# Scales carried between partitions by a DMA transpose instead of TensorE, in a three-stage kernel of attention and a Fourier mix

## The chip, the cores and the metric

One core of a Trainium2 chip. The metric is the device time of one execution, in microseconds (us). Engines are named as in the profile: PE is TensorE (PEld its weight loads), DVE is VectorE, ACT is ScalarE, POOL is GpSimd, and SP is the engine that issues nearly all DMAs, in the order of its own queue.

## The reference

Two independent results are concatenated. The first is a sliding-window attention over 2048 tokens with 32 heads of 32, the second a two-dimensional Fourier transform of another input, written as matrix products:

```python
qkv = (x @ wqkv)                                   # 2048 x 1024 by 1024 x 3072
scores = einsum("bhqd,bhkd->bhqk", q, k) * Dh**-0.5
mask = (i - j >= 0) & (i - j < 256)
a = (softmax(where(mask, scores, -1e9)) @ v) @ wo
re = x_B @ dft_hid_re.T;  im = x_B @ dft_hid_im.T
b = dft_seq_re @ re - dft_seq_im @ im              # 2048 x 2048 by 2048 x 1024
return concatenate([a, b], axis=-1)
```

All inputs are 32-bit floats.

## The kernel before

Every large product is done with 16-bit floats, three matmuls for one: an operand is multiplied by a scale, rounded to a high half, and what is left becomes a low half (`split`: ScalarE writes the high half, VectorE the low one). The scale is one number for a block of an operand, the reciprocal of a power of two just at or below its largest (or largest mean) absolute value. So ahead of each `split` four steps come:

- `top` (VectorE, a maximum) or `mean` (ScalarE, a sum of absolute values; `u_top` does the same for the Fourier matrices) leaves one number for each of the 128 partitions in `tops[key]`.
- `spread` takes the maximum over the pieces of a block, still one for each partition.
- `scale_of` brings the 128 numbers into every partition: a TensorE transpose of the column, repeated 128 times, against the identity `ident` writes a 128x128 tile `pt` in PSUM, and VectorE takes the maximum of its rows.
- three small operations on VectorE follow: keep the exponent (an `and` with 0x7F800000), bound and shift it, take the reciprocal.

The work goes in three stages. In the first, `order` lists 96 products (q, k and v of the attention, in chunks), and `tasks` lists by `at(n, ...)` what is written ahead of product n: loads, tops, scales, splits. `w_finish` is the scale and split of a block of the q or k weights, `wv_scale` and `wv_split` those of the v weights, `xp_step`, `scan_scale` those of the Fourier input and matrices and of the output weights. In the second stage 48 units of seven products each (`seven`, whose positions 0 to 6 use the PSUM banks a b a c a b a) do the Fourier transform: 16 of kind x, and 32 of kind c, whose operands `un_a`, `un_b`, `un_c` are split by `u_step` with the scale from `u_scale`. `u_top` runs two units ahead (turns 0 and 2), `u_scale` at the last turn of that unit. In the third stage the attention's output weights are applied.

Beside the first two stages the attention runs block by block (256 of them), fed by `tick`: `s_step` writes scores `s`, VectorE the row maximum `mx` and later the low half `hl`, ScalarE `bias`, the exponentials and the high half; one DMA transpose on SP turns `hl` into `t`, GpSimd masks it, and `v_step` multiplies it by v six blocks later.

TensorE's matmuls are chained in program order by `mm`. The order on the other engines is made when the kernel is built, by a scheduler with a model of times; `tc.issue_after(x)` pins an instruction behind another one on its engine. `behind[0]` is VectorE's latest low half of the attention, of q, k or v, or its latest addition in `seven`; `line[0]` is SP's latest transpose of `hl` or pinned load.

`pa` is the pool of the first stage; its tiles `yq` and `yv` (two buffers each) hold the results of q, k and v until their DMA has stored them.

Of the kernel before, what the change touches and what calls it, by code (L numbers as in the profile page):

```python
# [9 lines left out]
F32 = mybir.dt.float32  # L10
F32R = mybir.dt.float32r
F16 = mybir.dt.float16
BF16 = mybir.dt.bfloat16
U8 = mybir.dt.uint8
U32 = mybir.dt.uint32
AF = mybir.ActivationFunctionType
ALU = mybir.AluOpType
AX = mybir.AxisListType

P = 128  # L20
S = 2048
D = 1024
H = 32
# [5 lines left out]
CH = 512  # L29
NCH = S // CH  # L30
QB = CH // P
VW = 2 * DH + 2
# [8 lines left out]
VW = 2 * DH + 2  # L41
# [12 lines left out]
def fused_kernel(ctx: ExitStack, tc: tile.TileContext, xa, wqk, wv, wo, xb, wd, cs, out):  # L54
    nc = tc.nc
# [8 lines left out]
    const = ctx.enter_context(tc.tile_pool(name="const", bufs=1))  # L64
# [4 lines left out]
    ps_v = ctx.enter_context(tc.tile_pool(name="ps_v", bufs=1, space=PSUM))  # L69
# [8 lines left out]
    tsum = reg1[:, :7 * 8 * CH].rearrange("p (s h k c) -> p s h k c", s=7, h=2, k=4)  # L78
    spare = reg1[:, 7 * 8 * CH:]

    ident = const.tile([P, P], F32, name="ident")
    make_identity(nc, ident)


    upper = const.tile([P, P], F32, name="upper")
# [2 lines left out]
                            fill=0.0, base=0, pattern=[[1, P]], channel_multiplier=-1)  # L88
    upper2 = upper.bitcast(U32).unsqueeze(1).to_broadcast([P, 2, P])
    never = const.tile([P, 1], F32, name="never")  # L90
# [3 lines left out]
    pshift = const.tile([P, 1], F32, name="pshift")  # L94
    nc.gpsimd.memset(pshift, PSHIFT)

    nbank, units_on = [0], []

    def bank(name):
        nbank[0] += 1  # L100
        return ps_m.tile([P, CH], F32, tag=f"m{nbank[0] % 3}", name=name)
# [6 lines left out]

    junk = const.tile([P, ND * P], U8, name="junk")
    fixed = []  # L110
# [22 lines left out]
        return const.tile([P, 2], F32, name=f"sc_{name}")  # L133

    tops, head = {}, [True]


    behind = []
# [18 lines left out]
    def spread(key, n):  # L157
        t = tops.pop(key)
        if n > 1:
            t1 = small.tile([P, 1], F32, tag="top0", name=f"top1_{key}")  # L160
            vec(nc.vector.tensor_reduce, t1, t, axis=AX.X, op=ALU.max)
        else:
            t1 = t
        tops[key] = t1

    def scale_of(key, v, s, down=2.0 ** -14):

        if head[0]:
            pt = ps_s.tile([P, CH], F32, tag="s", name=f"pt_{key}")[:, :P]
            with tc.issue_after(fixed[0].ins) if fixed else nullcontext():  # L170
                fixed[:] = [nc.tensor.transpose(pt, tops.pop(key).to_broadcast([P, P]), ident)]
        else:
            pt = (ps_v.tile([P, CH], F32, tag="pv", name=f"pt_{key}") if units_on else bank(f"pt_{key}"))[:, :P]
            nc.tensor.transpose(pt, tops.pop(key).to_broadcast([P, P]), ident)
        vec(nc.vector.tensor_reduce, v, pt, axis=AX.X, op=ALU.max)
        vec(nc.vector.tensor_scalar, v.bitcast(U32), v.bitcast(U32), 0x7F800000, None, op0=ALU.bitwise_and)
        vec(nc.vector.tensor_scalar, v, v, 2.0 ** -100, down, op0=ALU.max, op1=ALU.mult)
        vec(nc.vector.reciprocal, s, v)
# [25 lines left out]
    line = []  # L204
# [193 lines left out]
    def at(n, f, *args):  # L398
        tasks.setdefault(n, []).append((f, args))
# [22 lines left out]
    def w_top(kd, g):  # L422
        mean(f"w{kd}{g}", wraw[kd, g].rearrange("p d t -> p (d t)"), 0, 1)
        spread(f"w{kd}{g}", 1)
# [126 lines left out]
    for (kd, g), n in use.items():  # L551
        if kd in "qk" and n >= 4:
            at(n - 6, w_load, kd, g)
            at(n - 4, w_top, kd, g)
            at(n - 3, w_finish, kd, g)
    for g in range(NG):
        at(max(use["q", g], use["k", g], 11), scores_scale, g)

# [3 lines left out]
        at(n, x_split, 0, (i,), behind_act)  # L562
    at(7, strict.__setitem__, 0, False)
    at(7, head.__setitem__, 0, False)
    at(4, x_top, 2, (0, 1))
    at(5, x_top, 2, (2, 3))
    at(7, x_finish, 2)
# [4 lines left out]
    at(11, x_known)  # L572
    at(11, wv_load, 0)
    at(14, wv_top, 0)
    at(15, wv_scale, 0)
    for i, n in enumerate((15, 16, 16, 17)):
        at(n, wv_split, 0, (i,))
    at(15, wv_load, 1)
    at(18, wv_top, 1)
    at(19, wv_scale, 1)  # L580
    for i, n in enumerate((19, 20, 21, 21)):
        at(n, wv_split, 1, (i,))
    at(20, wv_known)
    def scan(key, ns):
# [292 lines left out]
    at(len(order) - 3, x_left, 0, "c")  # L877


    with tc.tile_pool(name="pa", bufs=2) as pa:  # L880
        def qk_out(kd, g, c, ps, f):
            y = pa.tile([P, 2, CH], F16, tag="yq", name=f"y{kd}{g}_{c}")
            behind_act[:] = [nc.scalar.activation(y[:, 0], ps, AF.Copy, scale=f)]
            behind[:] = [vec(nc.vector.scalar_tensor_tensor, y[:, 1], ps, f, y[:, 0],
                             op0=ALU.mult, op1=ALU.subtract)]
            a = "qk".index(kd)
            nc.sync.dma_start(qk[g, c, a:a + 2, :, :, a].rearrange("j d h t -> (d h) j t"), y)
            nc.sync.dma_start(qk[g, c, 2 - 2 * a, :, :, a].rearrange("d h t -> (d h) t"), y[:, 0])

        def d_out(g):  # L890
            qk_out("q", g, 0, direct.pop(g), f0[:, g:g + 1])

        w_top("q", 0)
        x_top(0, (0, 1, 2, 3))
        d_mm(0, range(0, 4))
        w_scale("q", 0)
        d_mm(0, range(4, 8))
        w_top("q", 1)
        d_mm(1, range(0, 1))
        x_scale(0)  # L900
        d_known(0)
        d_mm(1, range(1, 3))
        w_scale("q", 1)
        d_known(1)
        d_out(0)
        w_split("q", 0)
        w_top("q", 2)
        d_mm(1, range(3, 8))
        x_top(1, (0, 1))
        d_out(1)  # L910
        d_mm(2, range(0, 2))
        w_scale("q", 2)
        d_known(2)
        x_top(1, (2, 3))
        d_mm(2, range(2, 8))
        w_top("q", 3)
        d_mm(3, range(0, 2))
        x_scale(1)
        x_split(1, (0, 1))
        d_out(2)  # L920
        d_mm(3, range(2, 4))
        w_scale("q", 3)
        d_known(3)
        x_split(1, (2,))
        d_mm(3, range(4, 8))
        x_split(1, (3,))
        w_split("q", 1)
        d_out(3)

        for n, (kd, g, c) in enumerate(order):  # L930
            if n < 4:
                continue
            if n == 22:
                first_cm.__exit__(None, None, None)
                att_cm = tc.tile_pool(name="att", bufs=2, side="right")
                cell["att"] = att_cm.__enter__()
                agen[0] = attention()
                upcoming[0] = next(agen[0])
            for f, args in tasks.pop(n, ()):
                f(*args)  # L940
            rate[0] = 2 * early * EARLY.get(n, 0.85) / 24
            ps = bank(f"p{kd}{g}_{c}")
            if kd == "v":
                t = c
                product(ps, lambda h, d: xin[:, t // 4, h, d, t % 4 * P:t % 4 * P + P],
                        lambda h, d: reg2[:, g, h, d])
                y = pa.tile([P, H // 2, VW], F16, tag="yv", name=f"yv{g}_{t}")
                nc.gpsimd.memset(y[:, :, DH:DH + 1], 1.0)
                nc.gpsimd.memset(y[:, :, 2 * DH + 1:], 0.0)
                f = vf[:, g, t // 4:t // 4 + 1]  # L950
                pv = ps.rearrange("p (h d) -> p h d", d=DH)
                behind_act[:] = [nc.scalar.activation(y[:, :, :DH], pv, AF.Copy, scale=f)]
                behind[:] = [nc.vector.scalar_tensor_tensor(y[:, :, DH + 1:2 * DH + 1], pv, f, y[:, :, :DH],
                                                            op0=ALU.mult, op1=ALU.subtract)]
                nc.sync.dma_start(vs[t, :, g * (H // 2) * VW:(g + 1) * (H // 2) * VW],
                                  y.rearrange("p h w -> p (h w)"))
            else:
                u = wun[kd, g]
                product(ps, lambda h, d: u[:, h, d], lambda h, d: xin[:, c, h, d])
                qk_out(kd, g, c, ps, DOWN if kd == "q" else kf[:, c:c + 1])  # L960
            if kd == "v" and g == 0 and c % 4 == 3:
                ready.add((0, c // 4))
            if kd == "v" and g == 1 and c == NT - 1:
                pass
            if kd == "k" and g > 0:
                ready.add((g, c))
# [116 lines left out]
            hook(pos)  # L1083


    units_on.append(True)
    perm, turns = [(nbank[0] + 1 + k) % 3 for k in range(3)], [0]
    with tc.tile_pool(name="pb", bufs=1) as pb:
        ybufs = [pb.tile([P, 2, CH], F32, name=f"y{k}") for k in range(3)]
        ybufs.append(spare[:, 16 * P:].bitcast(F32).rearrange("p (e c) -> p e c", e=2))  # L1090
        ny = [0]
# [11 lines left out]
        for r in range(4):  # L1103
            x0, c0 = 12 * r, 12 * r + 4
            for j in range(4):
                n = x0 + j
# [5 lines left out]
            for j in range(8):  # L1112
                n = c0 + j
# [20 lines left out]
        for n, (kind, p, c, i) in enumerate(units):  # L1134
# [35 lines left out]
            f = fu.pop(n)  # L1170
# [16 lines left out]
        for q in range(NT // 2):  # L1187
# [5 lines left out]
                  lambda t, y, at_=0: nc.sync.dma_start(out[t * P:t * P + P, at_:at_ + y.shape[1] * y.shape[2]],  # L1193
                                                        y.rearrange("p e c -> p (e c)")),
# [51 lines left out]
```

## Time and profile before

| | us |
|---|---|
| median of 3 runs | 1708.01 |
| lowest and highest | 1707.69, 1711.28 |
| the profiled execution | 1705.92 |
| its span, first to last instruction | 1703.9 |
| DVE, ACT, POOL busy | 1301.6, 1169.3, 573.8 |

The page also gives 348.62 MB moved by DMA, and a granted TensorE clock of 1.000 throughout. The busy time of PE is modelled from pipelined matmuls, whose durations overlap; the time that a matmul takes from the queue is read from the starts of its neighbours.

### The profile page before, as it was taken

What the parts mean: (1) busy time and instruction counts of PE and PEld (TensorE: products, weight loads), DVE (VectorE), ACT (ScalarE), POOL (GpSimd) and SP (SyncE); (2) the same over time, 40 slices, a digit from 0 to 9 for tenths busy, and PEclk for the clock granted to TensorE, in tenths of its full rate; (3) what the DMA queues carried; (4) which work ended last, traced back from release to release, by engine and by line L of the source; (5) the groups of instructions that cost most, each with busy time, mean ns of one, the idle gap of its engine ahead of it and who ended that gap; (6) DMA issues with size and microseconds to landing.
All of it is one profiled execution on the core that took longest, in us unless ns stands there. A gap on an engine that the chain in (4) does not pass through costs nothing.

```text
span 1703.9 us, 30860 instructions
## 1 busy us (share of the span) xinstructions
PE 1693.1 (99%) x10999; PEld 851.4 (50%) x10999; DVE 1301.6 (76%) x2225; ACT 1169.3 (69%) x2035; POOL 573.8 (34%) x874
## 2 busy tenths in 40 slices
PE   9999999999999999999999999999999999999999
PEld 4444555555555554555555555555555555444444
DVE  6847788887988688887678886688886698688442
ACT  4466666676877687888678886678877687563322
POOL 0000322334444341444423474433555425411000
PEclk9999999999999999999999999999999999999999
DMA  9747999999998995887998999986999976876431
GB/s 351 244 138 241 258 289 273 289 254 305 249 231 218 207 231 122 197 203 178 226 249 246 198 183 175 232 201 120 194 167 203 228 183 136 173 184 119 116 99 75
DMA packets 469898, 348.62 MB, mean 205 GB/s; under 512 B 376944, under 2 KB 409968, under 8 KB 468848
## 3 DMA queue, kind: packets, MB, share of 16 engines
q1 hardware_dynamic: 462064, 321.48, 75.3%
q0 software_dynamic: 7680, 25.17, 9.2%
q8 instruction: 86, 1.41, 0.4%
q14 instruction: 68, 0.56, 0.1%
HBM read 166.99 MB, written 106.17 MB: 160 GB/s over the span
## 4 chain that ended last, share of the span: by engine, by line
PE 80%; DVE 7%; ACT 4%; DMA 4%; issue 3%; POOL 2%; SPq 0%; DVEq 0%; POOLq 0%; ACTq 0%
PE p_a L114 22%; PE pv L114 13%; PE p_b L114 10%; PE pk L114 9%; PE pq L114 8%; PE p_c L114 5%; PE po_a L114 5%; PE s L114 3%; PE po_b L114 2%; PE far L114 1%; PE po_c L114 1%; DMA t<-hl 1%; DMA ots<-ot 1%; DVE reg L835 1%; DVE hl L270 1%
## 5 line engine op out<-in xcount | busy, mean ns | idle before, releaser
L266 ACT ACTIVATE s<-s,bias,escs 128x256 f32<-128x256 f32 (+1 forms) x512 | 270.0, 528 | 11.7
L284 POOL TENSOR_SCALAR_AFFINE_SELECT z<-t 128x512 f16<-128x512 f16 x224 | 187.0, 841 | 159.6 <-PE pv L114 142.3
L259 ACT ACTIVATE bias<-mx,pshift,escs 128x2 f32<-128x2 f32 x256 | 98.3, 384 | 171.6 <-DVE mx L256 171.3
L270 DVE TENSOR_TENSOR hl<-s,hl 128x512 f16<-128x512 f32 (+1 forms) x256 | 170.1, 665 | 56.0 <-ACT hl L269 55.2
L114 PEld LDWEIGHTS <-reg 128*128 128x128 f16 x1344 | 128.9, 97 | 141.7
L286 POOL TENSOR_SCALAR_AFFINE_SELECT t<-t 128x512 f16<-128x512 f16 x224 | 183.8, 829 | 11.4
L114 PE MATMUL p_a<-reg,un_c 128*128 128x512 f16 x768 | 181.2, 379 | 0.4 <-ACT p_c L1068 0.2
L263 POOL TENSOR_SCALAR mark<-bias 128x1 f32<-128x1 f32 x128 | 53.1, 415 | 363.0 <-ACT bias L259 356.5
L114 PE MATMUL pk<-reg,wu_k 128*128 128x512 f16 x768 | 174.4, 379 | 0.0
L256 DVE TENSOR_REDUCE mx<-s 128x2 f32<-128x512 f32 (+1 forms) x256 | 170.9, 668 | 3.4
L114 PE MATMUL pv<-reg,reg 128*128 128x512 f16 x768 | 172.7, 379 | 0.0
L114 PEld LDWEIGHTS <-un_c 128*128 128x128 f16 x1152 | 109.9, 97 | 121.3 <-issue 2.0
L114 PEld LDWEIGHTS <-un_b 128*128 128x128 f16 x1152 | 110.0, 97 | 117.8 <-issue 1.1
L114 PEld LDWEIGHTS <-un_a 128*128 128x128 f16 x1152 | 109.7, 97 | 116.3
L269 ACT ACTIVATE hl<-s 128x512 f16<-128x512 f32 (+1 forms) x256 | 148.8, 581 | 6.4 <-DMA t<-hl 1.0
L114 PE MATMUL pq<-reg,wu_q 128*128 128x512 f16 x672 | 151.3, 379 | 0.8 <-DVE reg L121 0.5
L114 PE MATMUL p_a<-reg,un_b 128*128 128x512 f16 x576 | 136.4, 379 | 0.4 <-DVE y L1036 0.3
L114 PE MATMUL p_b<-reg,un_b 128*128 128x512 f16 x576 | 136.4, 379 | 0.3 <-DVE reg L835 0.3
L114 PE MATMUL p_a<-reg,un_a 128*128 128x512 f16 x576 | 136.6, 379 | 0.0
L114 PE MATMUL p_c<-reg,un_a 128*128 128x512 f16 x576 | 136.5, 379 | 0.0
L254 DVE COPY_PREDICATED s<-upper,far 128x256 f32<-128x256 uint32 x224 | 94.3, 421 | 46.2 <-PE s L114 44.9
L114 PEld LDWEIGHTS <-qk 96*128 96x128 f16 x1056 | 87.9, 97 | 64.3 <-issue 1.8
(208 smaller groups left out, 3153.2 us busy)
## 6 DMA issues: line engine op xcount, KB each, us to landing
raw_u<-in_cs_dram SPq DMA_DIRECT2D x64, 512.0 KB, 4.9
qk<-qk SPq DMA_DIRECT2D x64, 384.0 KB, 4.9
out_dram<-y POOLq DMA_DIRECT2D x72, 256.0 KB, 6.1
raw_wd<-in_wd_dram SPq DMA_DIRECT2D x24, 512.0 KB, 5.2
vs<-yv SPq DMA_DIRECT2D x32, 264.0 KB, 4.4
vt<-vs SPq DMA_DIRECT2D x64, 132.0 KB, 4.5
raw_wo<-in_wo_dram SPq DMA_DIRECT2D x16, 512.0 KB, 8.1
qk<-yq SPq DMA_DIRECT2D x32, 256.0 KB, 3.4
```

The source lines that it names most:

```text
L114: fixed[:] = [nc.tensor.matmul(*args, **kwargs)]
L254: nc.vector.copy_predicated(s[:, :, P:], upper2, d["far"] if nb == 3 else never2)
L256: nc.vector.tensor_reduce(mx, sv, axis=AX.X, op=ALU.max, negate=True)
L259: nc.scalar.activation(bias, mx, AF.Identity, bias=pshift, scale=es)
L263: marks[:] = [nc.gpsimd.tensor_scalar(mark, bias[:, 0:1], 1.0, None, op0=ALU.mult)]
L266: nc.scalar.activation(sv[:, h], sv[:, h], AF.Exp, bias=bias[:, h:h + 1], scale=es)
L269: nc.scalar.activation(hi, sv, AF.Copy)
L270: behind[:] = [nc.vector.tensor_tensor(lo, sv, hi, op=ALU.subtract)]
L284: nc.gpsimd.affine_select(out=z, in_=pk, compare_op=ALU.is_gt, fill=0.0, base=0, pattern=[[0, 4], [-1, P]], channel_multiplier=1)
L286: nc.gpsimd.affine_select(out=pk, in_=pk, compare_op=ALU.is_ge, fill=0.0, base=0, pattern=[[0, 4], [1, P]], channel_multiplier=-1)
L835: nc.vector.tensor_tensor(lo, src, hi, op=ALU.subtract)
```

## The change

From product 11 of the first stage on, `scale_of` no longer uses TensorE. `spread` now also builds a tile `pb`: the upper 16 bits of each partition's number, of which the mask 0x7F80 keeps sign-free exponent bits only, repeated 128 times along the row. A DMA transpose on SP, pinned behind `line[0]`, writes it turned to `pc`. Later `scale_of` takes the maximum of the rows of `pc` (read as 16-bit powers of two), on VectorE, pinned behind `behind[0]`; the `and` falls away. The bound and the reciprocal stay. What comes before product 11 (the scales of the attention's input and of the first q weights) still goes over TensorE.

With it go some moves. `w_finish` of blocks used from product 16 on is listed two products ahead and not three; `wv_scale` and `wv_split` are listed one product later each. `yq` and `yv` become one tag `y` with three buffers in place of two and two. In the first stage `pb` and `pc` have three buffers, in the second one. `ident` lies in memory (`spare`) that is used for other things later.

```diff
+    crossing, crossed = [None], {}
 def spread(key, n):
 ...
         tops[key] = t1
+        if crossing[0]:
+            pb = crossing[0].tile([P, P], F16, tag="pb", name=f"pb_{key}")
+            nc.vector.tensor_scalar(pb.bitcast(U16), t1.bitcast(U16)[:, 1:2].to_broadcast([P, P]), 0x7F80, None,
+                                    op0=ALU.bitwise_and)
+            pc = crossing[0].tile([P, 1, P], F16, tag="pc", name=f"pc_{key}")
+            with tc.issue_after(line[0].ins) if line else nullcontext():
+                nc.sync.dma_start_transpose(pc, pb)
+            crossed[key] = pc.rearrange("p a t -> p (a t)").bitcast(BF16)
 def scale_of(key, v, s, down=2.0 ** -14):
+        if key in crossed:
+            with tc.issue_after(behind[0].ins):
+                nc.vector.tensor_reduce(v, crossed.pop(key), axis=AX.X, op=ALU.max)
+            nc.vector.tensor_scalar(v, v, 2.0 ** -100, down, op0=ALU.max, op1=ALU.mult)
+            nc.vector.reciprocal(s, v)
+            return
 ...
-            pt = (ps_v.tile([P, CH], F32, tag="pv", name=f"pt_{key}") if units_on else bank(f"pt_{key}"))[:, :P]
+            pt = bank(f"pt_{key}")[:, :P]
 ...
-            at(n - 3, w_finish, kd, g)
+            at(n - 3 if n < 16 else n - 2, w_finish, kd, g)
 ...
+    at(11, lambda: crossing.__setitem__(0, pa))
 ...
-    at(15, wv_scale, 0)
-    for i, n in enumerate((15, 16, 16, 17)):
+    at(16, wv_scale, 0)
+    for i, n in enumerate((16, 17, 17, 18)):
 ...
-    with tc.tile_pool(name="pa", bufs=2) as pa:
+    with tc.tile_pool(name="pa", bufs=3) as pa:
 ...
-            y = pa.tile([P, 2, CH], F16, tag="yq", name=f"y{kd}{g}_{c}")
+            y = pa.tile([P, 2, CH], F16, tag="y", name=f"y{kd}{g}_{c}")
 ...
     with tc.tile_pool(name="pb", bufs=1) as pb:
+        crossing[0] = pb
```

PE's order is otherwise what it was. In unit 4 of the second stage, where the scale of unit 6 is made, PE had the row with `pt_u` between the scores (`s`, `far`) and the products of the unit (`p_4_a`); before:

```order
L114 LDWEIGHTS qk_0_1_7729
L114 MATMUL s_8035<-qk_0_1_7729 128x128
L174 MATMUL pt_u_8073<-ident,top_u_7988 128x128
L114 LDWEIGHTS un_b
L114 MATMUL p_4_a<-reg_83,un_b 128x512
```

After, the same place on PE:

```order
L116 LDWEIGHTS qk_0_1_7754
L116 MATMUL s_8065<-qk_0_1_7754 128x128
L116 LDWEIGHTS un_b
L116 MATMUL p_4_a<-reg_83,un_b 128x512
L116 LDWEIGHTS un_b
```

The row has gone and nothing else has moved. VectorE at the same place (`y...<-p_4_b` is an addition of the unit, `mx` a row maximum of the attention), before:

```order
L1036 SCALAR_TENSOR_TENSOR y_6765<-p_4_b,fu_7712,y_6765 128x512
L254 COPY_PREDICATED s_8035<-upper,far 128x2x128
L121 TENSOR_REDUCE sc_u_8072<-pt_u_8073 128x1
L256 TENSOR_REDUCE mx_8043<-s_8035 128x2
L121 TENSOR_SCALAR sc_u_8072<-sc_u_8072 128x1 x2
L121 RECIPROCAL sc_u_8072<-sc_u_8072 128x1
```

After:

```order
L1054 SCALAR_TENSOR_TENSOR y_6789<-p_4_b,fu_7737,y_6789 128x512
L271 COPY_PREDICATED s_8065<-upper,far 128x2x128
L181 TENSOR_REDUCE sc_u_8102<-pc_u_8018 128x1
L273 TENSOR_REDUCE mx_8073<-s_8065 128x2
L182 TENSOR_SCALAR sc_u_8102<-sc_u_8102 128x1
L183 RECIPROCAL sc_u_8102<-sc_u_8102 128x1
```

The maximum stands where it stood, but takes `pc` from a DMA. SP there, after (`t_8008` is the transpose of a block's probabilities):

```order
L289 DMA_TRANSPOSE t_7892<-hl_7889 128x8x128
L289 DMA_TRANSPOSE t_8008<-hl_8005 128x8x128
L174 DMA_TRANSPOSE pc_u_8018<-pb_u_8016 128x1x128
L372 DMA ots<-ot_1_2_7674 128x512
L771 DMA raw_u_0_8086<-in_cs_dram 128x1024
```

The new transpose stands between a transpose of probabilities and the store and the loads that followed it. On ScalarE the scale is used by `un_a`; after:

```order
L276 ACTIVATE bias_8075<-mx_8073,pshift,escs 128x2
L129 ACTIVATE un_a<-raw_u_0_7863,sc_u_8102 128x1024
L283 ACTIVATE s_8065<-s_8065,bias_8075,escs 128x256
L349 ACTIVATE ohl_1_3_8144<-o_1_3_7936 128x256
L1086 ACTIVATE p_5_c<-p_5_a 128x512
```

Before, both halves of the exponentials stood here ahead of the copy `p_5_c`; now one does. In unit 31, where the scale of unit 33 is made, VectorE before:

```order
L254 COPY_PREDICATED s_15583<-upper,far 128x2x128
L256 TENSOR_REDUCE mx_15589<-s_15583 128x2
L121 TENSOR_REDUCE sc_u_15622<-pt_u_15623 128x1
L121 TENSOR_SCALAR sc_u_15622<-sc_u_15622 128x1 x2
L121 RECIPROCAL sc_u_15622<-sc_u_15622 128x1
```

After:

```order
L287 TENSOR_TENSOR hl_15568<-s_15554,hl_15568 128x512
L181 TENSOR_REDUCE sc_u_15671<-pc_u_15530 128x1
L273 TENSOR_REDUCE mx_15638<-s_15632 128x2
L182 TENSOR_SCALAR sc_u_15671<-sc_u_15671 128x1
L183 RECIPROCAL sc_u_15671<-sc_u_15671 128x1
```

Here the maximum has moved ahead of the attention's `mx`.

More of the change, by code (lines that the diff above doesn't have):

```diff
@@ L14 @@
 U8 = mybir.dt.uint8
+U16 = mybir.dt.uint16
 U32 = mybir.dt.uint32
@@ L79, in fused_kernel @@
     spare = reg1[:, 7 * 8 * CH:]
-    ident = const.tile([P, P], F32, name="ident")
+    ident = spare[:, :2 * P].bitcast(F32)
     make_identity(nc, ident)
@@ L95, in fused_kernel @@
     nc.gpsimd.memset(pshift, PSHIFT)
-    nbank, units_on = [0], []
+    nbank = [0]
     def bank(name):
@@ L579, in fused_kernel @@
     at(18, wv_top, 1)
-    at(19, wv_scale, 1)
-    for i, n in enumerate((19, 20, 21, 21)):
+    at(20, wv_scale, 1)
+    for i, n in enumerate((20, 21, 21, 22)):
         at(n, wv_split, 1, (i,))
@@ L946, in fused_kernel @@
                         lambda h, d: reg2[:, g, h, d])
-                y = pa.tile([P, H // 2, VW], F16, tag="yv", name=f"yv{g}_{t}")
+                y = pa.tile([P, H // 2, VW], F16, tag="y", name=f"yv{g}_{t}")
                 nc.gpsimd.memset(y[:, :, DH:DH + 1], 1.0)
@@ L1083, in seven @@
             hook(pos)
-    units_on.append(True)
     perm, turns = [(nbank[0] + 1 + k) % 3 for k in range(3)], [0]
     with tc.tile_pool(name="pb", bufs=1) as pb:
+        crossing[0] = pb
         ybufs = [pb.tile([P, 2, CH], F32, name=f"y{k}") for k in range(3)]
```

## The prediction

> **What bounds the kernel now.** I read the page first, then the waits of TensorE, then its timeline around one transpose. The page's engine row:
>
> ```profile
> span 1703.9 us, 30860 instructions
> PE 1693.1 (99%) x10999; PEld 851.4 (50%) x10999; DVE 1301.6 (76%) x2225; ACT 1169.3 (69%) x2035; POOL 573.8 (34%) x874
> ```
>
> Busy PE is modelled, so its 99% proves nothing alone. The longest waits of PE do; the columns are total us, times, longest:
>
> ```profile
> PE far L114 <- DVE s L254: 1.2, 1, 1.2
> PE s L114 <- DMA qk<-qk: 1.0, 1, 1.0
> ...
> PE pt_x L174 <- DVE top_x L121: 0.3, 1, 0.3
> ```
>
> These are single events of a microsecond in 1704, and only one of them is for a transfer. The timeline has the pace:
>
> ```profile
> 630.04 1.02 PE L114 MATMUL p_a<-reg,un_a 128*128 128x512 f16 x4
> ...
> 630.90 0.27 PE L174 MATMUL pt_u<-ident,top_u 128*128 128x128 f32 x1
> 630.91 1.50 PEld L114 LDWEIGHTS <-un_a 128*128 128x128 f16 x8
> 631.01 1.89 PE L114 MATMUL p_a<-reg,un_a 128*128 128x512 f16 x8
> ```
>
> From 630.04 to the transpose's start at 630.90 four matmuls start, one each 0.215 us. The matmul behind the transpose starts at 631.01, 0.11 us after it. So PE is a queue that stands still almost nowhere, and what is taken out of it shortens the run by its pace (0.11), not by its duration (0.27).
>
> **The change, part by part.** Removed from PE: the transposes of line 174 (all groups of them):
>
> ```profile
> L174 PE MATMUL pt_u<-ident,top_u x32: 272/272/275, 630.9 to 1515.8; 128*128 128x128 f32 x32
> L174 PE MATMUL pt_wk<-ident,top_wk x8: 273/273/275, 81.4 to 523.3; 128*128 128x128 f32 x8
> L174 PE MATMUL pt_xp<-ident,top_xp x8: 272/273/275, 124.3 to 324.8; 128*128 128x128 f32 x8
> L174 PE MATMUL pt_wq<-ident,top_wq x4: 273/274/303, 354.3 to 499.8; 128*128 128x128 f32 x4
> L174 PE MATMUL pt_x<-ident,top_x x2: 273/298/322, 50.7 to 72.1; 128*128 128x128 f32 x2
> L174 PE MATMUL pt_wv<-ident,top_wv x2: 273/273/273, 97.1 to 117.9; 128*128 128x128 f32 x2
> L174 PE MATMUL pt_wd<-ident,top_wd x2: 273/273/273, 336.3 to 391.3; 128*128 128x128 f32 x2
> L174 PE MATMUL pt_wo<-ident,top_wo x1: 303/303/303, 249.1 to 249.1; 128*128 128x128 f32 x1
> ```
>
> That is 59; the two of pt_x come before the switch and stay. 57 x 0.11 = 6.2 us go. By their whole duration (0.27) it would be 15.6, an upper end that the start of the next matmul excludes.
>
> Added on VectorE: 57 builds of `pb`, against 57 bit masks of the scale removed. A build has no row; the nearest are the 128x128 maximum and the 128x1 scalar operation (here two of them in 0.34 us):
>
> ```profile
> 668.18 0.28 DVE L121 TENSOR_REDUCE sc_u<-pt_u 128x1 f32<-128x128 f32 x1
> 1232.94 0.34 DVE L121 TENSOR_SCALAR sc_u<-sc_u 128x1 uint32<-128x1 uint32 x2
> ```
>
> So 0 to 57 x 0.14 = 8 us are added to 1302 busy us of an engine that is 24% idle; I take 0.1 each, 6 us, and nothing of it on the path.
>
> Added on SP and the DMA engines: 57 transposes. Of the two kinds that are there, `t` (4 or 8 blocks of 128 columns) has the first two rows, its issues on SP in ns and its time to landing; the last row is the landing of `ot`, with 4 blocks:
>
> ```profile
> L272 SPq DMA_TRANSPOSE t<-hl x256: 1188/1280/5102, 150.6 to 1458.9; - x128
> ...
> DMA to landing us min/median/max: 2.3/4.7/12.3
> DMA to landing us min/median/max: 1.7/4.0/8.7
> ```
>
> Issuing costs SP about 57 x 1.2 = 68 us, spread over the run. What stands behind it on SP are loads and the probabilities' transposes; the one wait of PE for a load above (1.0 us) says that these are early enough, so nothing is charged, with 2 us as the far end. A landing of one block I bound by 1.7 and 12.3 and take 4.0, the median of 4 blocks, since it queues behind the same transposes. The Trainium skill, in VectorE: DVE Perf Modes, section The three transpose paths, gives 390 ns for a 128x128 transpose on TensorE and 1309 ns through the DMA crossbar, and its Rules for kernel authors say to use TensorE where a PSUM result will do: by that the change adds 57 x 0.92 = 52 us. That holds where the transpose's length is on the path; here the trace shows 0.11 us of queue against a landing beside other work.
>
> So the question is who waits for the landing: the maximum stands in VectorE's fixed order, and everything behind it waits too. I laid the new order of VectorE and SP over the times of before. At most of the 57 places VectorE reaches the maximum 5 to 14 us after the issue, which hides 4.0. One such place, where the transpose comes right behind the first row and the maximum right behind the second:
>
> ```profile
> 878.77 0.42 SPq L355 DMA_DIRECT2D ots<-ot  x1
> ...
> 889.12 0.69 DVE L270 TENSOR_TENSOR hl<-s,hl 128x512 f16<-128x512 f32 x1 [0.41 <-ACT hl L269]
> ```
>
> Issue 879.2, maximum 889.8: 10.6 us. While units run, two places have no margin at all. The first:
>
> ```profile
> 667.34 1.23 SPq L272 DMA_TRANSPOSE t<-hl  x1
> 669.10 0.39 ACT L259 ACTIVATE bias<-mx,pshift,escs 128x2 f32<-128x2 f32 x1 [3.25 <-DVE mx L256]
> 670.55 1.14 ACT L127 ACTIVATE un_a<-raw_u,sc_u 128x1024 f16<-128x1024 f32 x1
> 673.43 0.62 ACT L1068 ACTIVATE p_c<-p_a 128x512 f32<-128x512 f32 x1
> 674.63 1.03 PE L114 MATMUL p_a<-reg,un_c 128*128 128x512 f16 x4
> ```
>
> The new transpose is issued behind this `t`, at 668.6, and lands at 672.6. The new maximum, which VectorE reaches at 668.3, stands ahead of `mx`; 0.3 for it and 0.6 for `mx` make 673.5 in place of about 669.0. Then ScalarE has, in its new order, `bias` (0.39), `un_a` (1.14), one half of the exponentials, `ohl` (0.5 each, an estimate between the first two for their width) and the copy `p_c` (0.62): 3.1 us, so the copy ends at 676.6 in place of 674.05. PE wants it at 674.63: a stall of 2.0 us. The second place:
>
> ```profile
> 1230.39 2.38 SPq L272 DMA_TRANSPOSE t<-hl  x1
> 1234.58 1.14 ACT L127 ACTIVATE un_a<-raw_u,sc_u 128x1024 f16<-128x1024 f32 x1
> 1236.35 0.59 ACT L1068 ACTIVATE p_c<-p_a 128x512 f32<-128x512 f32 x1
> 1238.59 2.75 PE L114 MATMUL p_a<-reg,un_c 128*128 128x512 f16 x12
> ```
>
> Issue 1232.8, landing 1236.8, `mx` 1237.7; `bias`, `un_a`, a half, the next `bias` and `p_c` are 3.0 us: 1240.7 against 1238.59, 2.1 us. Together 4.1 at a landing of 4.0; at 2.3, the shortest `t`, 0.7. One block is a quarter of `ot`, so I take 2.0, nearer the short end.
>
> Moved: scales of the later q and k weights by one product, those of v and their splits likewise. Two whole products (24 x 0.216 = 5.2 us each) still lie ahead of the use, and the chain behind the scale is short:
>
> ```profile
> 36.27 1.15 ACT L127 ACTIVATE wu_q<-raw_wq,scw 128x1024 f16<-128x1024 f32 x1 [1.59 <-DVE scw L121]
> 38.53 1.28 DVE L121 SCALAR_TENSOR_TENSOR wu_q<-raw_wq,scw,wu_q 128x1024 f16<-128x1024 f32 x1
> ```
>
> With 4.0 for a landing and 0.6 that is 7.0 of 10.4 us: nothing. The shared third buffer of `y` lifts one wait of ScalarE, behind which VectorE and then PE were late by 0.32 and 0.33 us:
>
> ```profile
> 46.83 0.60 ACT L883 ACTIVATE yq<-pq 128x512 f16<-128x512 f32 x1 [4.34 <-DMA qk<-yq]
> 50.69 0.32 PE L174 MATMUL pt_x<-ident,top_x 128*128 128x128 f32 x1 [0.32 <-DVE top_x L121]
> 51.34 1.89 PE L114 MATMUL pq<-reg,wu_q 128*128 128x512 f16 x8 [0.33 <-DVE yq L121]
> ```
>
> I take half, 0.3 of 0.65, the other end being 0. That GpSimd's fills for v now wait for the same buffers, and that the identity lies in memory used later, cost nothing: GpSimd is 34% busy, and the region is first written by the split that needs the last early transpose anyway.
>
> Sum: -6.2 - 0.3 + 2.0 = -4.5 us. The profiled execution took 1705.92 us (span 1703.9 and 2.0 around it) and would take 1701.4; it lies 2.1 below the median of the runs, 1708.01, so the forecast for a median is 1703.5. A change of 0.2%, 3.4 us, is about what a measurement of this kernel can tell from none.
>
> **Rivals.** (a) The waiting maximum eats the gain. For it: ScalarE already waits for VectorE's maxima more than for anything else, and in order:
>
> ```profile
> ACT bias L259 <- DVE mx L256: 171.3, 126, 4.2
> ```
>
> Against it: these 171 us reach PE as almost nothing. If the landings take 4.7, the two places cost 2.7 each (5.5), and five others, where I find margins of 1 to 4 us (near 945, 1026, 1400, 1418 and 1462), 0.2 each: 6.5, time 1708, the same. (b) The other side: the landings go with the load of the DMA engines (share, last column but one, here 0.93 from 30 to 630 us):
>
> ```profile
> 30.00:630.00 600.00, 597.79 (x3930) 301.86 (x3929) 470.12 (x813) 415.89 (x719) 179.07 (x318) 1.00 0.93 246
> ```
>
> A landing of 12.3 us in a gap of 8 holds VectorE 4.3, of which PE's banks absorb one or two. Slower by 3.4 us needs 9.9 us of new stalls, so four such landings; ten would give 1708 - 6.5 + 10 x 2.5 = 1726, and all 57 landings on the path 57 x 4.0 = 228 us more. Against it: 12.3 is the longest of 256. The Trainium skill's figures for the three transpose paths, above, speak for this side. (c) PE isn't the bound, its busy share being only pipelining, and what is taken out is filled by waiting for VectorE: time unchanged, 1708. Against it: the 0.216 pace holds right up to and behind the transpose. The Trainium skill, in Perfetto Trace Analysis, Identifying the Most-Contended Engine, says just this, that matmul busy share is a poor measure and the weight loads' share (here 50%) a better one, with the highest occupancy to be taken first, which here would be VectorE's.
>
> **How the numbers follow.** The forecast 0.60, (a) 0.26, (c) 0.04, (b) 0.10. That gives faster 0.60, same 0.30, slower 0.10. The range: 1700 is the sum without any new stall (-6.2 - 0.65 = -6.9, 1701.1) and a microsecond for the spread of the runs; 1710 takes in (a), (c) and the beginning of (b). The forecast's own range is 1701 to 1704.5.
>
> **What would show it.** After: PE with 57 fewer matmuls and no row of pt_u; busy PE lower by about 6 us; waits of `sc_u` for a DMA on VectorE, a few of 1 to 4 us; a landing near 4 us for `pc`; new waits of PE for `p_c` or VectorE of 2 us in all, near 674 and 1238. I am wrong if the waits of PE grow by more than 3 us, if `pc` lands in more than 5 us at the median, or if PE's gap at the places of the transposes stays.

## The result, and the profile after

| | before | after |
|---|---|---|
| median, us | 1708.01 | 1728.95 (1725.82 to 1731.12, five runs) |
| profiled execution, its span | 1705.92, 1703.9 | 1730.22, 1728.2 |

The ratio of after to before is 1.0119, 95% interval 1.0108 to 1.0131: slower by 1.2%, against a forecast of 0.3% faster. The ratios here and below leave out single executions that lie far above the others of their kernel (10215 us in e1, 1766 us in e2), which the medians still count. Here are the span and the engines' busy times of the page after:

```profile
span 1728.2 us, 30814 instructions
PE 1693.6 (98%) x10942; PEld 846.1 (49%) x10942; DVE 1305.6 (76%) x2225; ACT 1170.1 (68%) x2035; POOL 571.9 (33%) x874
```

The 57 transposes are gone from PE (10999 to 10942), yet the span is 24.3 us longer. Busy PE cannot show this; the waits of PE (line, total us, times, longest) do:

```profile
PE p_a L116 <- DVE y L1054: 8.2, 7, 2.3
PE far L116 <- DVE s L271: 6.7, 6, 2.0
PE p_a L116 <- ACT p_c L1086: 5.0, 2, 3.2
PE s L116 <- ACT hl L286: 2.6, 1, 2.6
```

Before, the longest total of a row was 1.2; all rows together give 6.5 us before and 30.1 after. The starts of the matmuls give the sum more closely. Give every shape one pace, the usual distance from its start to the next (0.216 us for 512 columns, 0.109 for a transpose and so on): the paces add up to 1686.0 us before and 1679.8 after, which is the 6.2 us of the forecast. What a start is later than its pace adds up to 10.0 us before and 40.3 after. -6.2 + 30.3 = 24.1, and the two profiled executions differ by 24.3. So 6.2 us of work left PE, and 30 us of new gaps came. How much of the 6.2 would be gained without the new gaps is a question for the experiments.

The chain of waits that ended last, shares of the span by engine, before and after:

```profile
PE 80%; DVE 7%; ACT 4%; DMA 4%; issue 3%; POOL 2%; SPq 0%; DVEq 0%; POOLq 0%; ACTq 0%
PE 68%; DVE 13%; DMA 7%; ACT 6%; issue 4%; POOL 1%; SPq 0%; DVEq 0%; ACTq 0%; POOLq 0%
```

VectorE waits for the landing of `pc` in eleven places. These are its waits, then the issues on SP for the units (ns, shortest, median and longest) and their median landing in us:

```profile
DVE sc_u L181 <- DMA pc_u<-pb_u: 15.0, 6, 4.2
DVE scw L181 <- DMA pc_wk<-pb_wk: 3.2, 2, 2.2
DVE vxp L181 <- DMA pc_xp<-pb_xp: 2.7, 2, 2.3
DVE vwd L181 <- DMA pc_wd<-pb_wd: 1.7, 1, 1.7
...
L174 SPq DMA_TRANSPOSE pc_u<-pb_u x32: 1119/1222/2373, 633.1 to 1535.7; - x32
...
pc_u<-pb_u SPq DMA_TRANSPOSE x32, 3.3
```

The landing is shorter than the forecast had it (3.3 against 4.0 at the median of the units), but the waits are 22.6 us. VectorE waited for scales before, too, when PE turned them: 8.9 us in ten places for `pt_u` alone, none longer than 1.5. This is the costliest of the new waits, in the timelines of SP, VectorE, ScalarE and PE (start, duration, engine and line; in brackets the idle time before):

```profile
1482.43 1.25 SPq L174 DMA_TRANSPOSE pc_u<-pb_u  x1
...
1483.64 0.74 DVE L1054 SCALAR_TENSOR_TENSOR y<-p_b,fu,y 128x512 f32<-128x512 f32 x1
1488.62 0.29 DVE L181 TENSOR_REDUCE sc_u<-pc_u 128x1 f32<-128x128 bf16 x1 [4.24 <-DMA pc_u<-pb_u]
...
1489.32 1.15 ACT L129 ACTIVATE un_a<-raw_u,sc_u 128x1024 f16<-128x1024 f32 x1 [5.57 <-DVE sc_u L183]
1490.38 0.58 ACT L1086 ACTIVATE p_c<-p_a 128x512 f32<-128x512 f32 x1
...
1491.01 1.24 PE L116 MATMUL p_a<-reg,un_c 128*128 128x512 f16 x5 [3.17 <-ACT p_c L1086]
```

SP issues the transpose at 1482.43; it lands 6.2 us after that, at 1488.6. VectorE reached its maximum at 1484.4 and stands. ScalarE's `un_a` needs the scale, and the copy `p_c`, which needs nothing of it, stands behind `un_a` in ScalarE's order. PE waits 3.2 us for `p_c`. Three in-order engines pass one late landing on.

### The profile page after: what moved, and what is told of

It is laid out like the page before. It is cut to its first block, busy times and chain, and to the rows that moved or that the text cites. A ratio compares the mean times of both kernels' runs of the same rounds, so it can differ in the third digit from the quotient of the medians.

```text
span 1728.2 us, 30814 instructions
## 1 busy us (share of the span) xinstructions
PE 1693.6 (98%) x10942; PEld 846.1 (49%) x10942; DVE 1305.6 (76%) x2225; ACT 1170.1 (68%) x2035; POOL 571.9 (33%) x874
## 2 busy tenths in 40 slices
DMA packets 479018, 350.49 MB, mean 203 GB/s; under 512 B 386064, under 2 KB 419088, under 8 KB 477968
## 4 chain that ended last, share of the span: by engine, by line
PE 68%; DVE 13%; DMA 7%; ACT 6%; issue 4%; POOL 1%; SPq 0%; DVEq 0%; ACTq 0%; POOLq 0%
PE p_a L116 19%; PE pk L116 9%; PE p_b L116 9%; PE pv L116 8%; PE pq L116 8%; PE po_a L116 5%; PE p_c L116 4%; DMA t<-hl 2%; PE po_b L116 2%; PE s L116 2%; DVE raw_u L810 2%; DVE hl L287 2%; DMA pc_u<-pb_u 1%; ACT s L283 1%; DVE mx L273 1%
## 5 line engine op out<-in xcount | busy, mean ns | idle before, releaser
L301 POOL TENSOR_SCALAR_AFFINE_SELECT z<-t 128x512 f16<-128x512 f16 x224 | 178.8, 805 | 164.6 <-PE pv L116 150.1
```

Source lines behind the costliest of these rows:

```text
L301: nc.gpsimd.affine_select(out=z, in_=pk, compare_op=ALU.is_gt, fill=0.0, base=0, pattern=[[0, 4], [-1, P]], channel_multiplier=1)
```

## The experiments

Each time is a median beside the kernel before on the same chip (1708.7 to 1710.8 in these groups); the ratio is to before, with its 95% interval.

| label | what is left of the change | us | ratio |
|---|---|---|---|
| e1_moves | the moves alone, scales over TensorE | 1709.4 | 1.0008 [0.9998, 1.0019] |
| e2_first_stage | DMA crossing in stage 1 only | 1717.7 | 1.0044 [1.0029, 1.0060] |
| e3_units | DMA crossing in stage 2 only, no moves | 1727.6 | 1.0111 [1.0072, 1.0150] |
| e4_no_landing | all, but nothing waits for the landing | 1716.1 | 1.0049 [1.0033, 1.0065] |
| e5_no_transpose | and no transpose is issued | 1706.6 | 0.9986 [0.9975, 0.9996] |
| e6_no_pb | and no `pb` is made | 1705.0 | 0.9980 [0.9970, 0.9990] |
| e7_pb_gpsimd | all, `pb` filled by GpSimd | 1723.5 | 1.0087 [1.0072, 1.0102] |
| e8_scale_later | all, unit scales one position later | 1747.6 | 1.0222 [1.0203, 1.0241] |
| e9_plain_copy | e4 with copies for transposes | 1711.0 | 1.0015 [1.0000, 1.0029] |
| e10_still_source | e4, SP does not wait for `pb` | 1717.8 | 1.0053 [1.0034, 1.0071] |
| e11_twice | e4, each transpose issued twice | 1767.1 | 1.0343 [1.0319, 1.0368] |
| e12_half_on_tensor | none: before, with 16-bit transposes on TensorE | 1705.6 | 0.9977 [0.9965, 0.9989] |
| e13_three_tiny | e4 with three 256-byte copies for each transpose | 1735.9 | 1.0160 [1.0134, 1.0187] |
| e14_act_queue | all, transposes issued by ScalarE | 1807.2 | 1.0572 [1.0545, 1.0599] |

Three theories stood first. W: VectorE's maximum waits for the landing, and what is queued behind it waits too. O: the moves, and the new order that the scheduler makes of them. S: 57 more transposes on SP and the DMA engines delay other transfers. Later came D (VectorE's own added work, `pb`, in its queue) and, inside S, S1 (SP stands until `pb` is made) and S2 (the issue and the transfer themselves).

**Which part.** e1 takes the crossing out and keeps every move:

```diff
+    ident = const.tile([P, P], F32, name="ident")
 ...
-    at(11, lambda: crossing.__setitem__(0, pa))
 ...
-        crossing[0] = pb
```

> All the moves of the change (scales of the first stage listed a product later, one tag y with three buffers) but every scale still over TensorE. Theory W (VectorE's maximum waits for a landing and holds what is queued behind it, down to TensorE): nothing waits for a landing, so 1706 to 1710, with waits of PE as before (about 7 us). Rival O (the moves and the new order that the scheduler makes of VectorE, ScalarE and SP cost the time, whatever lands when): 1715 or more. Rival S (57 more transposes on SP and the DMA engines delay other transfers): 1706 to 1710.

Measured 1709.4, 1.0008: the moves and the order they bring cost nothing that can be told. The order of the changed kernel itself is not in this run; e5, below, has nearly that order and is no slower than before, so that theory O falls by the two together.

e2 keeps the first of these `crossing` lines, e3 the second one (and undoes the moves).

> The DMA transposes in the first stage alone (25 of 57), the units' scales over TensorE. In the changed kernel about 13 us of PE's new waits lie before 630 us, though only 7.6 us of VectorE's waits for landings do. W: 1712 to 1719. O: as the moves alone, if those are the reason, else 1712 to 1719. S: about 25/57 of 21 us: 1717.

> The DMA transposes in the second stage alone (32 of 57), none of the moves of the first stage. W: 15 us of VectorE's waits for landings lie here, 1713 to 1721. O by the moves: 1708 or less. S: about 32/57 of 21 us: 1720.

1717.7 is in the range of both W and S, 1727.6 above both. Both stages lose, 0.44% and 1.11%; the sum, 1.55%, is above the whole loss of 1.19%, but the interval of e3 is wide. The loss is not at two places of the second stage, as the forecast had it.

**Wait or transfer.** In e4 the maximum reads `pb`, so a scale is that of each partition alone; the transposes are still issued and nobody waits for them:

```diff
-            crossed[key] = pc.rearrange("p a t -> p (a t)").bitcast(BF16)
+            crossed[key] = pb.bitcast(BF16)
```

> The changed kernel, but the maximum reads pb and not pc: the scales are then each partition's own and not the common ones; the 57 transposes are still issued and land, and nothing waits for them. The order of ScalarE and SP stays nearly that of the changed kernel. W: 1700 to 1706, as forecast for the change without waits, with PE's waits back at about 7 us. O: 1722 or more. S: 1722 or more.

TensorE's order is that of after; of VectorE's 2225 operations some 40 lie elsewhere. 1716.1 lies between the theories: waiting for the landing is 1.0119 - 1.0049 = 0.0070, 12 us of the loss, and 0.0049 remains in a kernel in which nothing waits for a landing. e5 then removes the DMA as well:

```diff
-            pc = crossing[0].tile([P, 1, P], F16, tag="pc", name=f"pc_{key}")
-                nc.sync.dma_start_transpose(pc, pb)
```

> Left out: the DMA transposes themselves; the maximum reads pb, the tile that VectorE made, so every scale is that of each partition alone. Orders of all engines but SP are those of the run without the wait for the landing (1716). Rival S (the 57 transposes on SP and the DMA rings hold up other transfers): 1702 to 1706, the rest of the loss goes with them. Theory D (VectorE itself: pb is queued ahead of additions that TensorE waits for with less than 0.5 us to spare): 1713 to 1717, no change against that run.

1706.6: the issued transposes, for which nothing waits, cost 1.0049 - 0.9986 = 0.0063, 10.8 us. That is theory S. The waits of PE in e4, and then in e5:

```profile
PE p_a L116 <- DVE y L1054: 6.5, 7, 2.2
PE far L116 <- DVE s L271: 3.3, 3, 1.7
PE s L116 <- DMA qk<-qk: 2.9, 1, 2.9
...
PE s L116 <- ACT s L280: 3.2, 1, 3.2
PE p_a L116 <- DVE y L1051: 1.5, 4, 0.5
```

The names of the releasers (VectorE's `y` and `s`) hide the cause, since VectorE has the same operations in the same order in the two kernels. Two places show how such a wait comes about. The first is in the first stage. SP in e4, then ScalarE and VectorE there:

```profile
383.04 1.22 SPq L174 DMA_TRANSPOSE pc_wk<-pb_wk  x1
...
386.80 0.40 SPq L239 DMA_DIRECT2D qk<-qk  x1
387.30 0.39 SPq L245 DMA_DIRECT2D vt<-vs  x1
387.78 1.23 SPq L289 DMA_TRANSPOSE t<-hl  x1
389.10 0.53 SPq L905 DMA_DIRECT2D qk<-yq  x1
389.68 0.50 SPq L906 DMA_DIRECT2D qk<-yq  x1
390.24 0.54 SPq L958 DMA_DIRECT2D wds<-wx  x1
...
395.75 1.15 ACT L129 ACTIVATE wx<-wx,vwd 128x1024 f16<-128x1024 f32 x1 [4.98 <-DMA wds<-wx]
...
396.93 1.28 DVE L123 SCALAR_TENSOR_TENSOR wx<-wx,vwd 128x1024 f16<-128x1024 f32 x1 [4.94 <-ACT wx L129]
398.14 0.42 DVE L271 COPY_PREDICATED s<-upper,far 128x256 f32<-128x256 uint32 x1
```

and the same in e5, which runs 2.9 us ahead here (its store `wds` before this one starts at 374.46, that of e4 at 377.37):

```profile
384.25 0.40 SPq L236 DMA_DIRECT2D qk<-qk  x1
384.75 0.54 SPq L955 DMA_DIRECT2D wds<-wx  x1
...
390.06 1.15 ACT L129 ACTIVATE wx<-wx,vwd 128x1024 f16<-128x1024 f32 x1 [0.91 <-DMA wds<-wx]
```

In e4 the store `wds` goes out at 390.24 instead of 384.75 + 2.9 = 387.65, 2.6 us later. ScalarE overwrites `wx` only when the store has read it, and waits 4.98 instead of 0.91; VectorE waits 4.94 behind it, and `s`, which PE's `far` needs, stands behind that: PE waits 1.1 us. But it is not the time of the transpose `pc_wk` that makes the store late: the copy `qk<-qk` starts at 386.80, no later than in e5 (384.25 + 2.9). What differs is the order of SP, made when the kernel is built: in e4 four other DMAs stand between this copy and the store, in e5 none.

The second place is in the second stage. A load on SP, then ScalarE, VectorE and PE in e4, and the first two of these rows in e5:

```profile
871.71 0.57 SPq L225 DMA_DIRECT2D raw_u<-in_cs_dram  x1
877.93 1.06 ACT L780 ACTIVATE junk<-raw_u 128x1024 uint8<-128x1024 f32 x1 [3.32 <-DMA raw_u<-in_cs_dram]
879.12 0.16 DVE L123 TENSOR_REDUCE top_u<-top_u 128x1 f32<-128x2 f32 x1 [2.66 <-ACT junk L780]
884.47 1.02 PE L116 MATMUL p_a<-wx,un_c 128*128 128x512 f16 x4 [2.15 <-DVE y L1054]
...
868.48 0.56 SPq L222 DMA_DIRECT2D raw_u<-in_cs_dram  x1
872.58 1.06 ACT L777 ACTIVATE junk<-raw_u 128x1024 uint8<-128x1024 f32 x1 [1.20 <-DMA raw_u<-in_cs_dram]
```

Here SP has the same order in both and issues the load at the same point (e5 is 3.2 us ahead). But the load lands 6.2 us after its issue in e4 and 4.1 in e5, and PE's wait of 2.15 follows from that. No transpose of a scale is issued between 838 and 884. At 1220 it is the same with a `t`, which lands after 10.9 us instead of 7.8; there one is issued 4 us ahead of it. Whether the added transposes made these landings longer or they are chance, one execution of each kernel does not tell. So the lateness reaches PE over two in-order engines in each case, but it starts from a changed order of SP in one place and from a long landing in another.

e6 also leaves out `pb`; the maximum reads each partition's own number, and VectorE has 57 rows of 0.22 us less, by which its busy time falls by 8.9 us.

> Left out: the transposes and the tile pb; the maximum reads the partition's own value. VectorE loses 57 times 0.22 us, 12.5 us of work in all, against the run before this one. Theory D, if it is the added work of pb: 1702 to 1706. If it is the new order of VectorE and ScalarE around the maximum and not the work: 1711 to 1717. Rival S: the same as the run without transposes.

1705.0 against 1706.6, with intervals that overlap (0.9970 to 0.9990, 0.9975 to 0.9996): VectorE's extra work is nearly free where nothing else is late. In e7 `pb` is filled by GpSimd, and the transposes and the waits for them stay:

> The full change, but pb is filled by GpSimd; VectorE only masks the one column (about 0.06 us instead of 0.22). Theory D (work of pb on VectorE): 1720 to 1725, since the waits for the landing stay and grow by GpSimd's copy (0.5 us or so). Theory W alone (waits for the landing are all of the loss): 1729 or a little above.

1723.5, in the range of theory D; 1.0087 against 1.0119, and the intervals do not meet. So about 5 us hang on `pb` when the landings are waited for. Whether it is the work or the order, of which some rows move with it, this run does not tell.

e8 gives the landing one position more:

```diff
-                do(n - 2, 6, u_scale, n)
+                do(n - 1, 0, u_scale, n)
-                for step, turn in enumerate((0, 1, 1, 2, 3, 4)):
+                for step, turn in enumerate((1, 2, 2, 3, 4, 5)):
```

> The full change, but in stage 2 the scale of a unit is called one position later (the first position of the next unit, 2.6 us on) and the six steps that use it one position later too. The landing gets 2.6 us more; it takes 3.3 us in the median. Theory W: the six waits of stage 2 of 15 us in all shrink to under 3 us, time 1716 to 1720, as in the run without the wait. Theory D: pb still ahead of the additions, so not below 1713. If the later steps make the operands late: 1725 and above, with waits of TensorE for un.

1747.6, a miss for both theories; the third case that the expectation names came. The operands became late (PE waits 5.0 us for VectorE's `un_b`), and the waits for `pc_u` did not shrink, one of them being 12.6 us:

```profile
DVE sc_u L181 <- DMA pc_u<-pb_u: 17.9, 3, 12.6
```

The run only says that a position later is too late for the splits.

**What of the issued transpose costs.** Four variants of e4, in which nothing waits for the landing. e10 reads a constant tile, so SP does not wait for `pb`; e9 issues a plain copy; e11 issues twice; e13 issues three copies of one row:

```diff
-                nc.sync.dma_start_transpose(pc, pb)
+                nc.sync.dma_start_transpose(pc, upper.bitcast(F16)[:, :P])          # e10
+                nc.sync.dma_start(pc[:, 0], pb)                                      # e9
+                nc.sync.dma_start_transpose(pc, pb); nc.sync.dma_start_transpose(pc, pb)   # e11
+                for r in range(3): nc.sync.dma_start(pc[32 * r:32 * r + 1, 0], pb[32 * r:32 * r + 1])  # e13
```

> As the run without the wait for the landing (1716), but the transposes read a constant tile, so that SP does not wait for pb. Theory S1 (SP held by the wait): 1705 to 1709. Theory S2 (issue time and DMA work of the transposes): 1713 to 1717.

1717.8 against 1716.1 of e4: SP's waiting for `pb` is not the cost, and S1 falls.

> As the run without the wait for the landing (1716), but a plain copy of pb to pc, of the same 32 KB, stands in place of each DMA transpose, at the same place of SP's queue and with the same wait for pb. Theory S1 (SP stands at these rows until VectorE has made pb, about 29 us in all, and everything queued behind is issued late): the wait stays, 1712 to 1717. Theory S2 (the transposes themselves: 1.2 us of SP for each and 14 us of all 16 DMA engines in all, where the DMA is full): a copy is shorter on both, 1705 to 1709.

> As the run without the wait for the landing (1716), but every DMA transpose is issued twice, one behind the other, into the same tile. Theory S2: the loss of 10 us against the run without transposes doubles: 1723 to 1729. Theory S1: the second transpose waits for nothing more, 1715 to 1718.

> As the run without the wait for the landing (1716), but three tiny copies of one row (256 bytes each) stand in place of each transpose, at the same place of SP's queue. SP is to be held about as long as by a transpose (three issues of 0.4 us or so against 1.22 us), the DMA engines hardly. If SP's time is the cost: 1713 to 1718. If the DMA engines' work is: 1705 to 1709. If both share it, in between, as with the plain copy of half SP's time and the same DMA work (1711).

1711.0 for e9 lies between its two ranges; 1767.1 for e11 and 1735.9 for e13 lie far above all of theirs and were misses. The packets and bytes of all DMAs in e5, e4 and e13 (e9 moves the 350.49 MB of e4), and then the issues on SP of e9 and e13 (e4 has the 1119/1222/2295 ns of a transpose):

```profile
DMA packets 469897, 348.60 MB, mean 205 GB/s; under 512 B 376944, under 2 KB 409968, under 8 KB 468848
...
DMA packets 479019, 350.49 MB, mean 204 GB/s; under 512 B 386064, under 2 KB 419088, under 8 KB 477968
...
DMA packets 475372, 348.68 MB, mean 202 GB/s; under 512 B 382416, under 2 KB 415440, under 8 KB 474320
...
L174 SPq DMA_DIRECT2D pc_u<-pb_u x32: 475/581/1701, 626.7 to 1517.0; - x32
...
L175 SPq DMA_DIRECT2D pc_u<-pb_u x96: 497/582/1414, 638.6 to 1540.3; - x96
```

Sorted by the time that the added issues take on SP (their count times a usual one), the loss against e5 is:

| | SP, us | added MB | against e5, by the ratios |
|---|---|---|---|
| e5 | 0 | 0 | 0 |
| e9 | 57 x 0.57 = 33 | 1.89 | +0.0029, 5 us |
| e4 | 57 x 1.22 = 70 | 1.89 | +0.0063, 11 us |
| e13 | 171 x 0.58 = 99 | 0.08 | +0.0174, 30 us |
| e11 | 114 x 1.22 = 139 | 3.77 | +0.0357, 61 us |

The row of e11 holds more than issues. Its second transpose writes the tile that the first one writes, and SP stands until the first has landed:

```profile
SPq L175 <- DMA pc_u<-pb_u: 55.6, 31, 12.5
```

With the scales of the first stage it is 84 us of standing, so the 61 us do not belong to 139 us of issues alone. The other rows rule out some causes. e13 moves next to nothing and costs nearly three times e4, so the bytes are not the price. e9 and e4 have the same number of DMAs and the same bytes, and the one with half of SP's time costs about half. SP's time fits all three, and from e4 to e13 the loss rises faster than it.

It is not shown alone, though. The order of SP's other 1127 DMAs moves with each variant: against e5 about 9 of them stand outside the common order in e9, 24 in e4, 52 in e13 and 65 in e11, which ranks the variants in the same way. Moved rows need not cost anything (in e1 24 moved against before, in e5 88, and neither is slower), but no run adds the issues and keeps the order. What is shown is that 57 issued transposes cost 11 us without any wait for their landing; that SP's time is the way is argued.

Nor is it a full queue. My sum of the durations of SP's DMA rows gives 72% of the time from 200 to 450 us before the change and 80% after it, with slices of 50 us up to 89%, but from 650 to 1500 us 52% and 56%. Of the 12 us by which e5's profiled execution is ahead of e4's at the end, only 3 are there when the second stage begins. The Trainium skill, in Perfetto Trace Analysis, section What "DMA-bound" means, says that a kernel can be bound by the DMA sequencer, where the issuing engine's track is solid with issues. Here the track is not solid in either stage, and the issued transposes cost time all the same.

e14 asks whether another queue would be free:

> The full change with the 57 transposes issued by ScalarE instead of SP. SP's time is as in before; the 68 us of issue and the wait for pb lie on ScalarE, which is 68% busy and copies the accumulators that TensorE needs back. If SP's time is the 11 us that the issued transposes cost and ScalarE has room: 1715 to 1720, the wait for the landing being left. If 1.2 us in front of a copy on ScalarE costs as much as in front of a load on SP or more: 1728 and above.

1807.2, but the run does not answer. On ScalarE's queue the transposes do not only take their 1.11 us; ahead of them stand waits, most of whose time is for transposes `t` that SP has in flight, up to 10 us each. SP waits in turn for the transposes of ScalarE, 114 us for those of the units and 151 in all:

```profile
L174 ACTq EVENT_SEMAPHORE  x107: 17/38/10147, 78.8 to 1612.7; - x107
L174 ACTq DMA_TRANSPOSE pc_u<-pb_u x32: 1110/1112/1722, 668.6 to 1612.8; - x32
...
SPq L289 <- DMA pc_u<-pb_u: 114.0, 20, 12.1
```

The Trainium skill, DMA: Bandwidth & Descriptors, DMA Transpose (X-bar), asks for this: transposes of two queues must not be in flight together. Whether the place of the issue alone would help stays open.

**A version that beats both.** What the change wanted from PE can be had without a DMA: the number is crossed as its upper 16 bits, still over TensorE, against a 16-bit identity. The mask stays after the maximum as it was, so VectorE does what it did.

```diff
-    ident = const.tile([P, P], F32, name="ident")
+    ident = const.tile([P, P], mybir.dt.bfloat16, name="ident")
 ...
-            nc.tensor.transpose(pt, tops.pop(key).to_broadcast([P, P]), ident)
+            nc.tensor.transpose(pt, tops.pop(key).bitcast(mybir.dt.bfloat16)[:, 1:2].to_broadcast([P, P]), ident)
```

(`pt` is the same bank, read as 16 bits.)

> A version that might beat both: the kernel before, with the scale still crossed over TensorE, but as the upper 16 bits of the maximum against a 16-bit identity, so that a transposition holds TensorE for the pace of a 128-column matmul of 16 bits (0.056 us in the records of before) instead of 0.109 us. Nothing is added to VectorE, SP or the DMA. 57 times 0.053 us is 3.0 us: 1705 to 1706, ratio 0.998 to 0.999, if TensorE is the bound and no place with a short margin moves; 1708 to 1710 if the new order of VectorE (some 65 rows) costs what is gained.

1705.6, 0.9977 [0.9965, 0.9989], within the range expected if TensorE is the bound. A transpose and the matmul behind it:

```profile
630.56 0.22 PE L174 MATMUL pt_u<-ident,top_u 128*128 128x128 bf16 x1
630.62 1.89 PE L114 MATMUL p_a<-reg,un_a 128*128 128x512 f16 x8
```

0.06 us from start to start instead of 0.11; the median over all 65 transposes is 0.056 against 0.109.

## Why the prediction was wrong, step by step

- *PE is a queue that stands still almost nowhere, and 6.2 us go.* The mechanism is right, the size was too large. The paces fell by 6.2, but with the rows gone and nothing put in their place (e6) the gain is 0.20%, 3.4 us (1.7 to 5.1 by the interval), with `pb` (e5) 2.4. In the profiled executions of the two, PE stands 3.5 and 3.2 us at one place near 412, where it stood 1.0 before. e12 turned 65 x 0.053 = 3.4 us of pace into 0.23%, 3.9 us (1.9 to 6.0).
- *The moves cost nothing.* Right, 1.0008 (e1). *Third buffer, -0.3*: the gaps of PE near 37 and 50 us add to 1.7 us before and 0.3 after, so 1.4, undersized and too small to tell in the runs.
- *`pb` 0.1 us each, nothing on the path.* A build takes 0.22 us, and with the masks gone VectorE's busy time grew by 4.0 us, not 6. Nothing on the path is right with no landing to wait for (e6); with it about 5 us hang on `pb`, by its work or by the order (e7).
- *SP: 68 us of issue, nothing charged, 2 us at the far end.* This step failed. The 70 us are there, and the issued transposes cost 10.8 us (e4 against e5). The reason given, that PE waits for a load only 1.0 us, looked at the last link only: a late store or load reaches PE through a wait of ScalarE, then of VectorE for ScalarE, and PE's row names VectorE. (The row of 1.0 us is for `qk`, the kernel's own results; the list has another of 0.9 for a load, of `wx` at the start.) The new order of SP was laid over the old times for the maxima, not for the stores and loads that it moves. Which part of the 10.8 us is SP's time, which the new order and which longer landings stays open.
- *New waits: two places, 2.0 us.* This step failed by a factor of six: 12 us (after against e4, 0.0070). The landing of 4.0 was on the safe side (3.3). What failed was the margin. The order of after was laid over the times of before, with the transposes issued when their row in SP's order came up; but SP itself was later, and single landings took up to 9.6 us. At 1488 the landing took 6.2 us and the maximum was reached 2.0 us after the issue; the forecast's 0.2 us of wait at a landing of 4.7 means 4.5. Six places of units waited, not two: the two named ones 0.9 and 0.3 us (at 677 and 1253), and those at 915, 962, 1488 and 1524 from 2.9 to 4.2. At 1488, the forecast's "near 1462" with 0.2 us, 3.2 us reached PE.
- *Rival (b), landings too long, slower, 0.10.* The sign was this one's, and its 2.5 us for each of ten landings (1726) came out near the time. By cause it holds for half: eleven waits with a mean of 2.1 us. The other half is the issued transposes.
- *Rival (a)*, the waiting maximum eats the gain: the mechanism of half the loss, at twice its 6.5 us. *Rival (c)*, PE not the bound, time unchanged: false, by e5, e6 and e12, though e5 and e6 gained only about half of the pace. By the ratios the terms are -2.4 (e5), 10.8 and 12 us, 20 in all, where the forecast had -6.5, 0 and 2.0.
- The Trainium skill's figure for the three transpose paths gave 52 us more, the trace's reading none; the runs show 21. A transpose's length was off PE, as the prediction says, but its landing and its issue were not off the path.
- *Wrong if the waits of PE grow by more than 3 us*: their rows grew from 6.5 to 30.1. That sign was the right one to name.

## What to carry to other kernels

Work taken from a full engine must go to a place with room, and an in-order DMA queue may have less than its busy share says: here 57 more issues cost 11 us, though SP was half to four fifths busy with issues. Count a DMA transpose as work on that queue (here 1.22 us for one block of 128 columns, 1.28 at the median for four or eight), and where a scheduler makes the orders, compare the new order of every queue with the old one, not only the times. A row of PE's waits names the last link; follow it back over two in-order engines before calling a queue's lateness harmless. When a step is only too dear, try to make it cheaper where it is (16 bits instead of 32) before moving it.

## What was not expected of the hardware

After some stalls PE runs slower for a while. Behind the wait of 2.6 us at 420 the next eight matmuls take 3.11 us instead of 1.89: from the fourth on they start 0.43 us apart, twice the usual pace. At 424 eight of them have 1.89 again. The last line is the stretch from 420 to 424 us, in which the granted clock (the third column from the end) was 0.59:

```profile
420.06 0.28 PE L116 MATMUL s<-qk 96*128 96x128 f16 x2 [2.62 <-ACT hl L286]
420.18 3.11 PE L116 MATMUL pk<-reg,wu_k 128*128 128x512 f16 x8
...
420.00:424.00 4.00, 3.94 (x31) 2.07 (x32) 2.60 (x4) 2.15 (x4) 0.20 (x1) 0.59 1.10 329
```

The starts show it in after at three places (behind 417, 917 and 974 us; 20 matmuls, 4.2 of the 30 us), and not behind the 3.3 us at 1487. The mean granted clock was 0.997, and 1.000 before. The Trainium skill, TensorE: Matmul & The Clock Gate, Part 1, gives a half clock after an idle window of about 3.4 us that runs freely. The halving agrees; but here single stalls of 2.8 (417) and 2.5 us (974) and a pair of 1.7 and 1.8 us (917) were enough. A stall of PE can thus cost more than its length.

A DMA of 256 bytes takes SP 0.58 us, the same as a plain copy of 32 KB (0.58, both at the median of the units); the transpose of 32 KB takes 1.22. The small copy is no cheaper for the queue.
